# Three layers fused on one core: other step counts in a weight preparation, four combinations on another engine, a first fetch three units later

## The chip, the cores and the metric

The program runs on one core of a Trainium2 chip. Its time is the device time of one execution in microseconds (us), the median of several; 830.21 us is the median of three runs of the kernel before (829.67 to 830.74). The engines are TensorE (PE in the rows, its weight loads PEld), VectorE (DVE), ScalarE (ACT), GpSimd (POOL) and SyncE (SP), which here issues nearly all DMAs. Each engine works through its own instructions in the order in which the program wrote them; between engines there are semaphores.

## The reference, cut to what matters

```
scores = q @ k^T / 8 ;  ret = scores * gamma[h]**(i-j) for i>=j, else 0 ;  x = ret @ v    # 4 batches, 8 heads, 576 tokens, 64 wide
h = x @ w_in  ; x = (h * tanh(log1p(exp(h)))) @ w_out       # 2304 tokens, 512 -> 2048 -> 512 (Mish)
h = x @ w_in2 ; y = (h * sigmoid(1.702 h)) @ w_out2         # the same sizes (GELU by a sigmoid)
```

All of it in float32. The kernel gets there with reduced-precision float32 products: every operand is split into a high part and the rest, and three products stand for one.

## The kernel before, in words

**Retention** (`attention`) goes over 20 units, a batch and a chunk of up to 128 tokens each, `u` = 0 to 19. A unit's q, k, v come by one DMA of 1 MB into one of six buffers. `scores(u)` multiplies q and k on TensorE and masks on VectorE (`pm`), `decay_v(u)` scales v by powers of gamma on GpSimd, `update` and `take` renew the state, `outputs` and `finish` give the unit's part of X, which stays in SBUF.

**The first layer** (`first_layer`) takes the first 768 tokens in 32 slots, and in the meantime converts the weights. They arrive as raw 64-bit numbers, a chunk `m` of 16 at a time: VectorE clamps (`clamp`), ScalarE rescales (`rest`, `rebase`), VectorE puts the sign in (`sign`), GpSimd joins (`join`), ScalarE makes the high part and VectorE the low one (`convert`). Two chunks are one round `r`; when its second is converted, `combine_first` makes four sums and differences of the round's quarters (tile `cy`), splits them too, and writes them to DRAM (`first_stream`) by DMA. The other tokens go through the same layer by seven instead of eight quarter products (lines 1105 to 1200), in two passes of 120 steps each, with operands read back from `first_stream` through a ring. The last product of a slot is waited for by an activation on ScalarE and a subtraction on VectorE.

**The preparation** of the second layer's weights runs beside those passes and the start of the second layer: 32 pieces (`prepare`), one begun every 6.5 steps, 14 in the first pass, 14 in the second, 4 in the second layer's first steps. A piece goes through the same stages as above and is written to the DRAM tile `stream`; its tiles are called `cr` (raw) and `cy` (the seven quarters), or `X` where they lie in a free part of X.

**What sets the order.** The order is written by hand. A job is a generator; `plan` gives it the position at which it begins, and `position(name, step)`, called at fixed places of each step, lets every job that waits at `name` go on to its next yield. A `yield "skip"` costs one step, `pause(n)` is `n` of them, and `yield "vector"`, `"act early"` or `"pool"` goes on at that engine's place of the same step or the next. So the number of skips between two stages is the number of steps by which the second stands later in its engine's queue. `EARLY_AT` gives the unit in which each of the first two chunks is fetched and that in which its conversion begins.

The helpers through which most instructions go have lines of their own in the rows: L132 is every ScalarE activation, L475 every VectorE `tt`, L141 and L213 `sign`, L201 `clamp`, L217 `join`, L270 the four combinations of `combine_first`, L342 those of `prepare`, L275 and L352 VectorE's low parts behind them, L851 `decay_v`, L1135 and L1072 the two passes' products, L671 and L720 the second layer's.

Of the kernel before, what the change touches and what calls it, by code (L numbers as in the profile page):

```python
# [14 lines left out]
ALU = mybir.AluOpType  # L15
# [3 lines left out]
B, H, S, D = 4, 8, 576, 64  # L19
# [29 lines left out]

KEPT = (0, 1, 2, 3, 4, 8, 9, 10, 11, 12)  # L50
X_UNITS = (4, 5, 6, 7, 10, 11, 12, 13)
EARLY_AT = ((0, 5), (7, 13))
EARLY = len(EARLY_AT)
LATE = [-2 + 1.95 * i for i in range(NM - EARLY)]
LENT = (2, 11, 12)
# [2 lines left out]
TABLES = NCH * H + NPAIR * (NCH + len(GROW) + GROW[0])  # L58
FIRST = 4 * DM + (TABLES + 15) // 16 * 16
REST = CH[-1][1]  # L60
LAST = 2 * NPAIR * REST + DM


# [36 lines left out]
def retention_mish_gelu_kernel(ctx: ExitStack, tc: tile.TileContext, qkv, w1, w2, first_unit, rests, out):  # L100
    nc = tc.nc
# [153 lines left out]
    def combine_first(r):  # L255

        live["first"] = 1
        c, w = r * NP, W[0, r]
        for p, h, q in ((1, 0, 0), (2, 0, 1), (4, 1, 1)):
            nc.sync.dma_start(  # L260
                out=first_stream[:, c + R_ORDER.index(p)],
                in_=w[:, h, :, q * 2 * P : (q + 1) * 2 * P].bitcast(F32),
            )
        a11, a12, a21, a22 = (words(held[0, r])[3][:, q] for q in range(4))
        both = temp[0].tile([P, 8, 2 * P], F32R, tag="cy", name="cy")
        hi, y = both[:, :4], both[:, 4:].bitcast(F32)
        at = R_ORDER.index(6)
        s1, s2, s3, s4 = (y[:, R_ORDER.index(p) - at] for p in (5, 6, 7, 3))
        for o, a, b, op in ((s1, a21, a22, ALU.add), (s3, a11, a21, ALU.subtract), (s2, s1, a11, ALU.subtract), (s4, a12, s2, ALU.subtract)):
            nc.gpsimd.tensor_tensor(out=o, in0=a, in1=b, op=op)  # L270
        yield "pool"
        yield "act early"
        act(hi, y)
        yield "vector"
        nc.vector.tensor_tensor(out=both[:, 4:], in0=y, in1=hi.bitcast(F32), op=ALU.subtract)  # L275
        for j, t in enumerate((hi.bitcast(F32), y)):
            nc.sync.dma_start(out=first_stream[:, c + at : c + at + 4, j], in_=t)
        yield "vector"
        live["first"] = 0

    def pause(n):

        for _ in range(n):
            yield "skip"

    def prepare(j, r, part, half):

        late_one = j - sum(PREPARED_IN[:2])
        s = 0 if late_one >= 0 else R_ROUNDS[j >= PREPARED_IN[0]]
        while live["cr"] == 3:  # L290
            yield "skip"
        live["cr"] += 1
        if late_one >= 0:
            raw = idle(0, late_one % 3 * 2 * DM, 2 * DM)
        elif j % 3 == 2:
            raw = idle(s, 4 * DM, 2 * DM)
        else:
            raw = keep.tile([P, 2 * DM], F32, tag=f"x{2 + j % 3}", name="cr")
        raw = raw.rearrange("p (q n) -> p q n", q=4)
        nc.sync.dma_start(out=raw.bitcast(I32), in_=w2[r, part, half].bitcast(I32))  # L300
        yield from pause(7)
        yield "vector"
        clamp(raw)
        yield "act early"
        rest(raw)
        yield "act early"
        rebase(raw, nc.scalar)
        yield "skip"
        yield "vector"
        sign(raw)  # L310
        yield "pool"
        while live["cy"] == 3:
            yield "pool"
        live["cy"] += 1
        order = (UP_ORDER, DOWN_ORDER)[part]
        n = NP * 2 * P
        if late_one == 3:
            y = idle(0, 2 * DM, n).bitcast(F32R)
        elif late_one in (0, 1):
            at = NM - 2 + late_one  # L320
            y = place(at).tile([P, n], F32R, tag=f"w{at}", name="cy")
        elif late_one == 2 or j % 3 == 1:
            y = keep.tile([P, n], F32R, tag="side", name="cy")
        elif j % 3 == 0:
            y = temp[0].tile([P, n], F32R, tag="cy", name="cy")
        else:
            y = idle(s, 0, n).bitcast(F32R)
        y = y.rearrange("p (o a n) -> p o a n", a=2, n=P)
        v = y[:, :, 1].bitcast(F32)
        a11, a12, a22, s1, s2, s3, s4 = (order.index(p) for p in (1, 2, 4, 5, 6, 7, 3))  # L330
        a21 = s3

        bits = y[:, :, 1].bitcast(I32)
        join(raw[:, 0:2], bits[:, a11 : a21 + 1 : a21 - a11])
        join(raw[:, 2:4], bits[:, a12 : a22 + 1 : a22 - a12])
        for o, a, b, op in (
            (s1, a21, a22, ALU.add),
            (s3, a11, a21, ALU.subtract),
            (s2, s1, a11, ALU.subtract),
            (s4, a12, s2, ALU.subtract),  # L340
        ):
            nc.gpsimd.tensor_tensor(out=v[:, o], in0=v[:, a], in1=v[:, b], op=op)  # L342
        yield from pause(3)
        live["cr"] -= 1
        yield "skip"
        yield "act early"

        hi = y[:, :, 0]
        act(hi, v)
        yield from pause(2)  # L350
        yield "vector"
        nc.vector.tensor_tensor(out=y[:, :, 1], in0=v, in1=hi.bitcast(F32), op=ALU.subtract)  # L352
        yield from pause(2)
        c, step = (r * NP, 1) if part == 0 else (UP_STEPS + r, NR)
        nc.sync.dma_start(
            out=stream[:, c : c + (NP - 1) * step + 1 : step, half],
            in_=y.rearrange("p o a n -> p o (a n)").bitcast(F32),
        )
        prepared.add((r, part, half))
        yield from pause(8)  # L360
        live["cy"] -= 1

    n_u = len(UNITS)
# [8 lines left out]

    for m, (loaded_in, converted_in) in enumerate(EARLY_AT):
        plan("fetch", loaded_in - n_u, fetch(m))
# [410 lines left out]
    def attention():  # L785
        with tc.tile_pool(name="att", bufs=1) as ap:
# [11 lines left out]
            def load(u):  # L798

                b, c = UNITS[u]  # L800
                if c == NCH - 1:
                    t = ap.tile([P, LAST], F32, tag="rest", name="rest", bufs=2)
                    nc.sync.dma_start(out=t, in_=rests[b])
                    loaded[u] = views(t, REST)
                    return
# [9 lines left out]
            for t in (state[1][:, 0], state[1][:, 1:]):  # L815
# [6 lines left out]
            vt = tab[:, : NCH * H].rearrange("p (c h) -> p c h", c=NCH)  # L822
# [10 lines left out]
                out=cm, in_=cm, pattern=[[1, P]], compare_op=ALU.is_ge, fill=0.0, base=0, channel_multiplier=-1  # L833
# [13 lines left out]
            def decay_v(u):  # L847
                b, c = UNITS[u]
                n = CH[c][1]
                vv = loaded[u][2][:n].rearrange("p (h d) -> p h d", d=D)  # L850
                nc.gpsimd.tensor_tensor(  # L851
                    out=vv, in0=vv, in1=vt[:n, c, :].unsqueeze(2).to_broadcast([n, H, D]), op=ALU.mult
                )

            def scores(u):
                n = CH[UNITS[u][1]][1]
# [77 lines left out]
            def finish(u, o):  # L934
# [4 lines left out]
                while part < n:  # L939
# [6 lines left out]
                    )  # L946
                    part += w

            scores(0)
            decay_v(0)  # L950
            act(gt[:, 0, :, : GROW[0]], first)
            for j, w in enumerate(GROW):
                for p in range(NPAIR):
                    act(gt[:, 0, p, w : 2 * w], gt[:, 0, p, :w], scale=grow[:, p, j : j + 1])
            for u in range(n_u):
                step = u - n_u
                if u - 1 in wide and wide.index(u - 1) + len(buffers) < len(wide):
                    n = wide[wide.index(u - 1) + len(buffers)]
# [14 lines left out]
                o = outputs(u, before)  # L973
                if u == 1:
                    scores(u + 1)
                if u < NCH - 1:
                    n = CH[u + 1][1]
# [286 lines left out]
```

## Time and profile before

| what | value |
|---|---|
| median of three runs | 830.21 us |
| profiled execution: its own time, its span | 833.2 us, 831.5 us |
| TensorE matmul busy | 808.3 us, 97% of the span |
| VectorE, ScalarE, GpSimd busy | 582.3, 444.2, 220.3 us |
| mean granted TensorE clock | 0.995 |
| DMA | 219.67 MB, 264 GB/s |

The span begins with the first instruction and ends with the last. TensorE's sum is busy for all but some 23 us, so the rows to read are those on its waits. The stages lie in the span so: retention from 0 to about 73 us, the first layer's first 768 tokens to about 200, the two passes to 474, the second layer to the end. A wait of several semaphores is put down to the one that came last.

### The profile page before, as it was taken

To read this page: it belongs to the slowest core of one execution; us is meant where nothing else is said; L and a number is where in the kernel's file an instruction comes from. 1 tells how busy PE (TensorE), PEld (TensorE's weight loads), DVE (VectorE), ACT (ScalarE), POOL (GpSimd) and SP (SyncE) were. 2 spreads that over 40 slices of the span, in tenths; PEclk is the share of its full clock that TensorE was granted. 3 is DMA by queue.
4 is the path that set the end of the run, shared out by engine and by line. 5 is a ranking of instruction groups with operands and counts; after the bars stand their busy time and mean duration, and the time that the engine had idled before them with its cause. 6 is when DMAs were issued, how large, how long until landed. Compare 5 with 4: busy or idle time off the path is not lost.

```text
span 831.5 us, 14152 instructions
## 1 busy us (share of the span) xinstructions
PE 808.3 (97%) x5392; PEld 762.5 (92%) x5392; DVE 582.3 (70%) x959; ACT 444.2 (53%) x861; POOL 220.3 (26%) x284
## 2 busy tenths in 40 slices
PE   8999999999998999999899998999999999999998
PEld 8898888888887998988789998999999999999998
DVE  4786999999565667366476577588655798455776
ACT  5445776676655566555665554456233664233542
POOL 3452565652355550155463023000000000000000
PEclk9999999999999999999999999999999999999999
DMA  9983577838778886588787499878877778877775
GB/s 360 420 342 118 194 253 250 275 114 258 261 272 281 304 289 230 181 297 290 274 309 249 164 314 352 296 246 281 307 247 259 255 263 278 294 245 261 253 265 168
DMA packets 86132, 219.67 MB, mean 264 GB/s; under 512 B 5808, under 2 KB 51888, under 8 KB 78768
## 3 DMA queue, kind: packets, MB, share of 16 engines
q1 hardware_dynamic: 85920, 218.56, 76.1%
q8 instruction: 43, 0.70, 0.3%
q10 hardware_dynamic: 144, 0.20, 0.1%
q14 instruction: 25, 0.20, 0.1%
HBM read 169.98 MB, written 48.76 MB: 263 GB/s over the span
## 4 chain that ended last, share of the span: by engine, by line
PE 50%; POOL 7%; ACT 5%; DVE 5%; DMA 3%; issue 1%; SPq 0%; POOLq 0%; DVEq 0%
PE p L720 21%; PE p L671 18%; PE acc L1072 6%; PE p L1135 5%; POOL cy L342 3%; POOL cy L217 2%; ACT X L132 2%; DMA ring<-first_stream 2%; POOL X L342 2%; ACT cy L132 1%; DMA ring<-stream 1%; ACT cr L132 1%; POOL X L217 1%; DVE cr L141 1%; DVE cy L352 1%
## 5 line engine op out<-in xcount | busy, mean ns | idle before, releaser
L671 PE MATMUL p<-xop,ring 128*128 128x384 f32 x1008 | 176.1, 334 | 3.6 <-DVE cs L475 2.1
L671 PEld LDWEIGHTS p<-xop,ring 128*128 128x128 f32 x1008 | 174.7, 188 | 4.5 <-DVE cs L475 4.5
L720 PE MATMUL p<-g,ring 128*128 128x384 f32 x1008 | 175.2, 334 | 0.0
L720 PEld LDWEIGHTS p<-g,ring 128*128 128x128 f32 x1008 | 174.8, 188 | 0.0
L1072 PE MATMUL acc<-g,w 128*128 128x512 f32 (+1 forms) x768 | 145.7, 339 | 1.3 <-DVE g L475 1.3
L1072 PEld LDWEIGHTS acc<-g,w 128*128 128x128 f32 x768 | 125.5, 190 | 19.1 <-DVE g L475 2.0
L1135 PE MATMUL p<-xop,ring 128*128 128x384 f32 x672 | 131.3, 340 | 9.3 <-ACT c L132 4.0
L1135 PEld LDWEIGHTS p<-xop,ring 128*128 128x128 f32 x672 | 115.4, 188 | 13.7 <-DVE c L475 6.0
L132 ACT ACTIVATE g<-cs 128x384 fp32r<-128x384 f32 x168 | 79.0, 517 | 60.3 <-PE p L720 60.0
L475 DVE TENSOR_TENSOR g<-cs,g 128x384 fp32r<-128x384 f32 x168 | 90.0, 554 | 26.7 <-ACT g L132 25.0
L132 ACT ACTIVATE cs<-cs 128x384 f32<-128x384 f32 x72 | 37.7, 526 | 106.2 <-DVE cs L475 106.1
L475 DVE TENSOR_TENSOR g<-c,g 128x384 fp32r<-128x384 f32 x64 | 39.5, 617 | 52.2 <-ACT g L132 52.1
L437 PE MATMUL acc<-g,w 128*128 128x512 f32 (+1 forms) x384 | 72.3, 337 | 0.0
L437 PEld LDWEIGHTS acc<-g,w 128*128 128x128 f32 x384 | 60.2, 190 | 7.6
L217 POOL TENSOR_TENSOR raw<-raw 128x512 int32<-128x512 int32 x32 | 38.1, 1190 | 74.9 <-DVE raw L213 60.3
L132 ACT ACTIVATE cy<-cy 128x896 fp32r<-128x896 f32 (+1 forms) x30 | 29.5, 982 | 46.5 <-POOL cy L342 27.6
L475 DVE TENSOR_TENSOR cs<-cs 128x384 f32<-128x384 f32 x96 | 53.4, 557 | 0.8
L342 POOL TENSOR_TENSOR cy<-cy 128x128 f32<-128x128 f32 x88 | 52.3, 604 | 5.2
L132 ACT ACTIVATE g<-c 128x384 fp32r<-128x384 f32 (+1 forms) x96 | 50.5, 526 | 3.9 <-PE acc L437 0.9
L217 POOL TENSOR_TENSOR cy<-cr 128x256 int32<-128x256 int32 x38 | 29.3, 791 | 77.8 <-DVE cr L213 70.6
L416 PE MATMUL h<-x,w 128*128 128x512 f32 x192 | 46.6, 392 | 0.9 <-ACT c L132 0.9
L132 ACT ACTIVATE raw<-raw 128x512 int32<-128x512 uint32 x64 | 41.4, 677 | 10.8 <-DVE raw L201 10.4
(92 smaller groups left out, 998.3 us busy)
## 6 DMA issues: line engine op xcount, KB each, us to landing
ring<-stream SPq DMA_DIRECT2D x112, 512.0 KB, 4.6
ring<-stream SPq DMA_DIRECT2D x28, 1024.0 KB, 4.8
stream<-cy SPq DMA_DIRECT2D x22, 896.0 KB, 4.6
raw<-w_dram SPq DMA_DIRECT2D x32, 512.0 KB, 7.7
unit<-qkv_dram SPq DMA_DIRECT2D x15, 1024.0 KB, 10.8
ring<-first_stream SPq DMA_DIRECT2D x14, 1024.0 KB, 7.0
ring<-first_stream SPq DMA_DIRECT2D x28, 512.0 KB, 6.0
cr<-w_dram SPq DMA_DIRECT2D x19, 512.0 KB, 5.7
```

The lines of the kernel that those rows point to most:

```text
L132: nc.scalar.activation(out=o, in_=i, func=f, scale=scale, bias=bias)
L141: nc.vector.scalar_tensor_tensor(out=o, in0=i0, scalar=s, in1=i1, op0=op0, op1=op1)
L217: nc.gpsimd.tensor_tensor(out=o, in0=upper, in1=bits, op=ALU.add)
L342: nc.gpsimd.tensor_tensor(out=v[:, o], in0=v[:, a], in1=v[:, b], op=op)
L352: nc.vector.tensor_tensor(out=y[:, :, 1], in0=v, in1=hi.bitcast(F32), op=ALU.subtract)
L416: nc.tensor.matmul(h[:, :n], lhsT=W[0, m // 2][:, m % 2, a, k * P : (k + 1) * P], rhs=xs[t, k][:, b, :n], start=((k, a, b) == order[0]), s ...
L437: nc.tensor.matmul(acc[t, e][:, :n], lhsT=W[1, m // 2][:, m % 2, a, e * P : (e + 1) * P], rhs=g[:, b, :n],  start=(begins(i) and a == 0 an ...
L475: eng.tensor_tensor(out=o, in0=a, in1=b, op=op)
L671: nc.tensor.matmul(banks[p], lhsT=w[:, k, a * P : (a + 1) * P], rhs=x[:, b, k], start=(p not in SAME and k == 0 and a == 0 and b == 0), st ...
L720: nc.tensor.matmul(banks[e, p], lhsT=w[:, e, a * P : (a + 1) * P], rhs=g[:, b], start=(p != 2 and r == 0 and a == 0 and b == 0), stop=(r = ...
L1072: nc.tensor.matmul(acc[t, e][:, :w], lhsT=W[1, m // 2][:, m % 2, a, e * P : (e + 1) * P], rhs=g[:, b, o : o + w], start=(m == 0 and a == 0 ...
L1135: nc.tensor.matmul(bank, lhsT=w[:, a, k * P : (k + 1) * P], rhs=x[:, b, k], start=(p in (1, 2, 7) and k == 0 and a == 0 and b == 0), stop= ...
```

## The change

It has five parts. (1) `EARLY_AT`: the first chunk of weights is fetched at unit 2 instead of 0 and converted from unit 8 instead of 5. (2) `decay_v` of unit 0 is shared: five heads (320 columns) on VectorE and three (192) on GpSimd, and it is written ahead of `scores(0)`. (3) `combine_first`: its four combinations are VectorE's, and the `yield "pool"` behind them is gone. (4) `prepare`: 6 skips instead of 7 between the fetch and the clamp; 2 instead of 1 between ScalarE's rescaling and VectorE's sign; 5 instead of 3 behind GpSimd's combinations (with the one that stays, 6 instead of 4 up to ScalarE's split); 1 instead of 2 between ScalarE's split and VectorE's low part; 7 instead of 8 up to the buffer's release. (5) A constant `SPLIT` for part 2, by which the lines below it move by one.

```diff
-EARLY_AT = ((0, 5), (7, 13))
+EARLY_AT = ((2, 8), (7, 13))
+SPLIT = 5
@@ combine_first
-            nc.gpsimd.tensor_tensor(out=o, in0=a, in1=b, op=op)
-        yield "pool"
+            nc.vector.tensor_tensor(out=o, in0=a, in1=b, op=op)
         yield "act early"
@@ prepare
-        yield from pause(7)
+        yield from pause(6)
         yield "vector"
         clamp(raw)
...
         rebase(raw, nc.scalar)
-        yield "skip"
+        yield from pause(2)
         yield "vector"
         sign(raw)
...
-        yield from pause(3)
+        yield from pause(5)
         live["cr"] -= 1
         yield "skip"
         yield "act early"
         hi = y[:, :, 0]
         act(hi, v)
-        yield from pause(2)
+        yield "skip"
         yield "vector"
         nc.vector.tensor_tensor(out=y[:, :, 1], in0=v, in1=hi.bitcast(F32), op=ALU.subtract)
         yield from pause(2)
...
-        yield from pause(8)
+        yield from pause(7)
         live["cy"] -= 1
@@ decay_v
-                nc.gpsimd.tensor_tensor(
-                    out=vv, in0=vv, in1=vt[:n, c, :].unsqueeze(2).to_broadcast([n, H, D]), op=ALU.mult
-                )
+                for eng, h, e in ((nc.vector, 0, SPLIT), (nc.gpsimd, SPLIT, H)) if u == 0 else ((nc.gpsimd, 0, H),):
+                    by = vt[:n, c, h:e].unsqueeze(2).to_broadcast([n, e - h, D])
+                    eng.tensor_tensor(out=vv[:, h:e], in0=vv[:, h:e], in1=by, op=ALU.mult)
@@ attention
+            decay_v(0)
             scores(0)
-            decay_v(0)
```

TensorE's order does not change. SyncE's queue during retention, from the load of unit 4 (`rest`) on; `unit` tiles are retention's buffers, `raw` the first chunk of weights. Before:

```order
L803 DMA rest<-rests_dram 128x1024
L811 DMA unit<-qkv_dram 128x2048
L183 DMA raw<-w_dram 128x512 x2
L811 DMA unit<-qkv_dram 128x2048
L811 DMA unit_77<-qkv_dram 128x2048
L811 DMA unit_78<-qkv_dram 128x2048
```

Now:

```order
L803 DMA rest<-rests_dram 128x1024
L811 DMA unit<-qkv_dram 128x2048 x2
L811 DMA unit_77<-qkv_dram 128x2048
L811 DMA unit_78<-qkv_dram 128x2048
L803 DMA rest<-rests_dram 128x1024
L184 DMA raw<-w_dram 128x512 x2
```

The two fetches of the first chunk stood ahead of the load of unit 6 and of three loads behind it; now they stand behind unit 9's.

ScalarE's queue at the first two preparations of the first pass; `cr` and `X` of 128x512 are the two rescalings of a piece, `cy` of 128x7x128 its split, `c` and `g` belong to the first layer. Before:

```order
L132 ACTIVATE c<-p 128x384
L132 ACTIVATE cy<-cy 128x7x128
L132 ACTIVATE cr<-cr 128x512 x2
L132 ACTIVATE c<-p 128x384
L132 ACTIVATE c<-c 128x384
L132 ACTIVATE g<-c 128x384
L132 ACTIVATE c<-p 128x384
L132 ACTIVATE cy<-cy 128x7x128
L132 ACTIVATE X<-X 128x512 x2
```

Now:

```order
L133 ACTIVATE cr<-cr 128x512
L133 ACTIVATE c<-p 128x384
L133 ACTIVATE cr<-cr 128x512
L133 ACTIVATE cy<-cy 128x7x128
L133 ACTIVATE c<-p 128x384
L133 ACTIVATE c<-c 128x384
L133 ACTIVATE g<-c 128x384
L133 ACTIVATE X<-X 128x512
L133 ACTIVATE c<-p 128x384
L133 ACTIVATE X<-X 128x512
L133 ACTIVATE cy<-cy 128x7x128
```

The rescalings of the next piece stood behind the split of the piece ahead of it, and now stand in front of it.

VectorE's queue in the first layer, at the first round's combinations; L457 makes the low part of an activation, L249 that of a weight. Before:

```order
L457 TENSOR_TENSOR g<-c,g 128x256
L249 TENSOR_TENSOR w_1190<-raw,w_1190 128x512
L141 SCALAR_TENSOR_TENSOR raw<-raw 128x512
L213 TENSOR_SCALAR raw<-raw 128x512
L201 TENSOR_SCALAR raw<-raw 128x512
L457 TENSOR_TENSOR g<-c,g 128x512
L275 TENSOR_TENSOR cy<-cy 128x1024
```

Now:

```order
L457 TENSOR_TENSOR g<-c,g 128x256
L271 TENSOR_TENSOR cy<-raw 128x256 x2
L271 TENSOR_TENSOR cy<-cy,raw 128x256
L271 TENSOR_TENSOR cy<-raw,cy 128x256
L250 TENSOR_TENSOR w_1191<-raw,w_1191 128x512
L142 SCALAR_TENSOR_TENSOR raw<-raw 128x512
L214 TENSOR_SCALAR raw<-raw 128x512
L202 TENSOR_SCALAR raw<-raw 128x512
L457 TENSOR_TENSOR g<-c,g 128x512
L275 TENSOR_TENSOR cy<-cy 128x1024
```

Four instructions of 256 columns are added to VectorE in each of eight rounds, between two low parts of activations, and GpSimd's queue loses them.

## Rows read from the trace of the kernel before

**Rows 1.** TensorE by stretch: stretch, length, busy (matmuls), granted clock, DMA share, GB/s
```profile
8.00:60.00 52.00, 50.14 (x938) 0.97 0.98 403
60.00:200.00 140.00, 138.83 (x923) 1.00 0.61 200
...
206.00:320.00 114.00, 109.53 (x608) 0.99 0.82 284
...
346.00:430.00 84.00, 78.74 (x439) 1.00 0.80 281
...
480.00:530.00 50.00, 46.44 (x265) 1.00 0.97 351
530.00:828.00 298.00, 297.89 (x1719) 1.00 0.77 260
```
**Rows 2.** TensorE's waits, 206 to 430 us: total, times, longest
```profile
PE p L1135 <- DVE c L475: 3.9, 9, 0.9
PE p L1135 <- ACT c L132: 3.1, 4, 1.1
PE p L1135 <- DMA ring<-first_stream: 1.5, 2, 0.9
PE acc L1072 <- DVE g L475: 1.3, 2, 0.7
```
**Rows 3.** TensorE by stretch, columns as in Rows 1
```profile
24.00:30.00 6.00, 6.00 (x86) 0.72 1.01 419
266.00:272.00 6.00, 5.37 (x22) 0.72 0.96 335
```
**Rows 4.** Timeline of retention: start, length, engine, what, [idle before <- releaser]
```profile
4.14 1.06 SPq L183 DMA_DIRECT2D raw<-w_dram  x2
...
5.93 1.29 DVE L866 TENSOR_TENSOR pm<-sc,cm 128x512 f32<-128x512 f32 x2 [4.47 <-PE sc L862]
...
7.18 0.69 PE L885 MATMUL ds<-unit 128*64 128x64 f32 x16 [1.35 <-POOL unit L851]
...
23.99 1.21 PE L862 MATMUL sc<-unit 64*128 64x128 f32 x16 [1.61 <-DMA unit<-qkv_dram]
```
**Rows 5.** Timeline of the first layer, and VectorE's 256-column group (mean ns)
```profile
150.60 1.34 DVE L141 SCALAR_TENSOR_TENSOR raw<-raw 128x512 int32<-128x512 int32 x1
...
153.48 1.06 ACT L132 ACTIVATE cy<-cy 128x1024 fp32r<-128x1024 f32 x1 [3.19 <-POOL cy L270]
...
156.57 0.68 DVE L141 SCALAR_TENSOR_TENSOR raw<-raw 128x512 int32<-128x512 int32 x1
...
156.76 3.02 PE L416 MATMUL h<-x,w 128*128 128x512 f32 x12 [0.90 <-ACT c L132]
...
L403 DVE TENSOR_TENSOR side<-X,side 128x256 fp32r<-128x256 f32 x4 | 1.8, 462 | 0.0
```
**Rows 6.** Waits of ScalarE and VectorE, 206 to 430 us
```profile
ACT cy L132 <- POOL cy L342: 22.1, 16, 3.4
...
ACT X L132 <- POOL X L342: 10.0, 6, 3.4
...
DVE cy L352 <- ACT cy L132: 8.9, 7, 1.9
...
DVE X L352 <- ACT X L132: 4.7, 4, 1.9
```
**Rows 7.** Timeline of the first pass at one such wait
```profile
261.45 0.95 ACT L132 ACTIVATE cy<-cy 128x896 fp32r<-128x896 f32 x1 [3.39 <-POOL cy L342]
...
264.90 1.33 PE L1135 MATMUL p<-xop,ring 128*128 128x384 f32 x6 [1.08 <-ACT c L132]
```
**Rows 8.** Second layer's start: TensorE's waits 480 to 530 us, then the timeline
```profile
PE p L671 <- DVE cs L475: 2.1, 2, 1.4
PE p L671 <- DMA ring<-stream: 1.5, 1, 1.5
...
501.18 0.69 DVE L141 SCALAR_TENSOR_TENSOR X<-X 128x512 int32<-128x512 int32 x1 [1.16 <-ACT X L132]
```

## The prediction

> **What bounds the kernel now.** I read TensorE by stretch first, since its sum is busy for 97% of the span. From 530 to 828 us it is busy for 297.89 of 298 us [rows 1]: nothing can be won there. What it loses lies in four places: 1.9 us from 8 to 60 us, 1.2 us from 60 to 200, 4.5 us from 206 to 320 and 5.3 us from 346 to 430 (the two passes), and 3.6 us from 480 to 530 (the second layer's start) [rows 1]; each is length less busy. To these comes the clock. In two stretches of six us the mean granted clock is 0.72 [rows 3]: part of each ran at the lower level, 1.2 GHz, and 6 x 0.28 = 1.7 us of work at 2.4 GHz were lost in each. Both follow on idle time of TensorE, the first on the 1.61 us at 23.99 us [rows 4], the second on the 1.08 us at 264.90 us [rows 7] and another short wait behind it.
>
> Next come the waits, to see who ended that idle time. In retention it is a DMA, unit 6's load [rows 4]. In the two passes 3.9 + 3.1 + 1.3 = 8.3 us are put down to VectorE's and ScalarE's work on activations and 1.5 us to ring loads [rows 2]; in the second layer 2.1 us to VectorE and 1.5 us to a ring load [rows 8].
>
> The engines behind them are not short of time there but stand in line. ScalarE waits 22.1 + 10.0 = 32.1 us, in 22 cases, for GpSimd's combinations in front of a piece's split [rows 6]. One case shows what this does: ScalarE sits idle for 3.39 us, the activation parts queued behind it come late, and TensorE sits idle for 1.08 us until one of them is there [rows 7]. Since the next piece's rescaling also stands behind that split, its sign, its join and its combinations come late too, and the piece after meets the same wait.
>
> **The change part by part.** The sum is made against the profiled execution, 833.2 us with a span of 831.5; that lies 3.0 us above the median of 830.21, and I take the sum off the median.
>
> *First chunk later.* Two fetches of 512 KB are issued at 4.14 us, ahead of unit 6's load [rows 4]. DMA moves 403 GB/s in this stretch, at a share of 0.98 [rows 1], so the 1.05 MB take 2.6 us out of unit 6's way. It is awaited for 1.61 us [rows 4]: the wait goes, with 1.0 us to spare, and units 7 to 9 come earlier by the same 2.6 us. Without this idle time I expect the clock not to fall: 1.7 us. Together 3.3 us (0 to 3.3). What is moved: the two DMAs, and for each of them eight instructions of the conversion, four of VectorE, three of ScalarE and one of GpSimd. They now lie between units 8 and 12, whose VectorE work is lighter because the first split of X is over; the second chunk begins at unit 13 as before. The DMAs are queued ahead of unit 10's load as they were, so from there on nothing comes later. Cover is needed on VectorE alone: were it gone, one unit's mask (1.29 us [rows 4]) would be late.
>
> *Unit 0's decay shared.* TensorE waits 1.35 us for it, to 7.18 us [rows 4]. 320 columns on VectorE take about 0.5 us, between 0.46 for 256 and 0.68 for 512 columns [rows 5]. But VectorE now does this ahead of the two masks, which last 1.29 us from 5.93 us [rows 4] and cannot begin before the tables have landed: they end about 0.6 us later, at 7.8 us, and the outputs need them. What the state gains, the outputs wait for. I take 0 (0.5 lost to 0.5 won): units 1 to 3 land behind one another and set the pace anyway.
>
> *Combinations on VectorE.* Added to VectorE: 8 rounds x 4 x 0.46 us [rows 5] = 14.8 us, in the stage where it has hardly any idle time. Against it: beside GpSimd's combinations the same VectorE instruction lasts 1.34 us and alone 0.68 [rows 5]. Per round two instructions of this kind stand beside them, 1.3 us, and two shorter ones, so that 1.3 us or somewhat more come back for 1.85 us added. ScalarE's wait of 3.19 us in front of the split, which made TensorE wait 0.90 us [rows 5], becomes one for VectorE's 1.85 us. I take all of the 1.2 us lost in the stage [rows 1] as won, and no loss, as TensorE's products use an activation only three slots after it was made. From both sides: 1.2 us won to 14.8 lost.
>
> The Trainium skill (SBUF — State Buffer, "Who interferes with whom") has it that a VectorE instruction with two SBUF inputs contends with a GpSimd instruction that reads SBUF, and that the loser blocks in full. The rows agree on the contention but show a doubling, 1.34 against 0.68 us. By the rule VectorE would get back all of GpSimd's time and gain on the whole; by the rows it loses about 0.5 us a round, and as TensorE does not wait for it there, the sum is the same.
>
> *Preparation.* In steps of about one product group, GpSimd now has six instead of four before ScalarE asks, and the next piece's rescaling is in front of the split. A step is about 1.1 us (274 us for two passes of 120 steps), two steps more are 2.3 us, and the 22 waits are 1.5 us in the mean [rows 6]; the longest, 3.4 us, come from a piece that was itself late. So I take it that the 32.1 us of ScalarE's waiting go. One wait may stay: VectorE's low part has one step instead of two behind the split, and it already waited 8.9 + 4.7 = 13.6 us with two [rows 6]. Of the two kinds of waiting, 32.1 of 45.7 us go, 0.70, and I take that share of TensorE's 8.3 us: 5.8 us (0 to 8.3). The ring loads stand behind the write of a piece on SyncE, and that write waits for the low part; with the low part on time I take half of the 1.5 us [rows 2], 0.7 (0 to 1.5). The second stretch at a low clock goes with its wait: 1.7 us (0 to 1.7). A fetch now has six steps to land instead of seven, a reason not to take more.
>
> *Second layer's start.* The wait at 501.18 us, VectorE's sign for a rescaling that stood behind the split [rows 8], is of the same kind and made the longer of the two waits, 1.4 us [rows 8]; it goes, the shorter one, VectorE's own backlog, stays. The ring load that TensorE waited 1.5 us for [rows 8] stood behind the last piece's write on SyncE; in the new order it stands ahead of it, and I take the 1.5 us as won. Together 2.8 us (0 to 3.6).
>
> Sum: 3.3 + 0 + 1.2 + 5.8 + 0.7 + 1.7 + 2.8 = 15.5 us, so **814.7 us**. With every wait gone (3.3 + 1.2 + 8.3 + 1.5 + 1.7 + 3.6 = 19.6, and 0.5 of unit 0) it would be 810.1.
>
> **The rivals.** *Waits that change places.* VectorE's low part, now one step behind, waits for ScalarE at every piece and holds the activation parts behind it; the passes give back a third of the 8.3 us, the low clock stays, as do the ring loads, and the second layer gives half. 3.3 + 1.2 + 2.8 + 1.4 = 8.7: 821.5 us. For it: 11 such waits, up to 1.9 us, with two steps [rows 6]. Against it: those came behind a split that was itself late.
>
> *Nothing arrives.* Retention's 3.3 us are taken back at the first layer, which needs weights that are loaded when retention's buffers come free, and the passes are bound by ring loads, at a DMA share of 0.82 [rows 1], so that activation waits turn into DMA waits: 829 to 831 us. Against it: from 530 to 828 us TensorE has no wait with ring loads at a share of 0.77 [rows 1].
>
> *VectorE becomes the first layer's bound, and the kernel slower.* Nothing of the contention comes back, the added 1.85 us per round reach TensorE in all 8 rounds (14.8 us), and each such wait, about as long as the 1.61 us of retention, is followed by 1.7 us lost to the clock, as there (13.6 us). Less the other gains, 14.3 us, this is 14.1 us slower: 844.3 us. It decides from the point where VectorE's work of a round is longer than TensorE's, so that the lag of three slots is used up. For it: VectorE's idle time in this stage is small; against it: the doubling [rows 5], which shows that part of its busy time is waiting for GpSimd. The Trainium skill (Perfetto Trace Analysis, "Optimizing Scalar/DVE Operations") warns that moving work between these two engines might not help as they share a port; no row here shows the moved work.
>
> **How the numbers follow.** Forecast 0.66, around 809.5 to 819; changed places 0.20, 819 to 826; nothing 0.07; slower 0.07. What a measurement can tell from no change is about 0.2%, 1.7 us. Faster: 0.66 + 0.20 and a little of the third, 0.87; same 0.06; slower 0.07. The range runs from the end where every wait is gone, a little below it, to the upper end of the second case: 809 to 826.
>
> **What would show it.** In the profile after: unit 6's scores without a wait and a clock of 1.00 from 24 to 30 us; no ScalarE wait for L271 over 2 us and TensorE busy throughout 60 to 200 us; ScalarE's waits for GpSimd's combinations in the passes under 8 us instead of 32; TensorE's waits from 206 to 430 us under 4 us and a clock of 1.00 around 266 us; no wait for a ring load near 528 us. I am wrong if VectorE's waits for ScalarE's split grow beyond 14 us, if low parts of activations come later than three slots in the first layer, or if the time won in retention shows again as a wait of the first slots.

## The result, and the profile after

Median of the kernel after: 811.07 us (810.31 to 812.1, four runs); of the kernel before beside it: 830.48 us (829.67 to 832.0, four runs). The ratio is 0.9765, with an interval of 0.9747 to 0.9783, that is 19.5 us less (18.0 to 21.0). The forecast was 814.7 us in a range of 809 to 826. The profiled execution took 810.9 us with a span of 809.2; against the profiled execution of before that is 22.3 us less, some 3 us more than by the medians, since that execution of before (833.2 us) was itself 2.7 us above this median; it held two stretches at the lower clock [rows 3].

TensorE by stretch in the kernel after (stretch, length, busy, granted clock, DMA share, GB/s), to be read against [rows 1]:

```profile
8.00:60.00 52.00, 51.95 (x1000) 1.00 0.98 403
60.00:200.00 140.00, 140.00 (x893) 1.00 0.66 213
206.00:320.00 114.00, 113.96 (x652) 1.00 0.85 288
346.00:430.00 84.00, 82.14 (x469) 1.00 0.91 309
480.00:530.00 50.00, 48.81 (x279) 1.00 0.91 328
530.00:806.00 276.00, 275.60 (x1590) 1.00 0.78 261
```

The stretches in which TensorE lost time are nearly full, and what is left sits in two of them: 1.9 us from 346 to 430 and 1.2 us from 480 to 530. Who is waited for there is read from TensorE's waits, first 206 to 430 us, then 480 to 530 us (total, times, longest), to be read against [rows 2, 8]:

```profile
PE p L1135 <- DMA ring<-first_stream: 1.9, 1, 1.9
...
PE p L671 <- DMA ring<-stream: 0.8, 1, 0.8
PE p L671 <- DVE cs L475: 0.4, 1, 0.4
```

Of 15 waits for VectorE and ScalarE in the two passes none is left. Of ring loads one wait is left, and it is longer than the two of before together (1.9 us instead of 1.5).

*Retention.* SyncE's first chunk, the start, and unit 6's scores in the timeline after, against [rows 4]:

```profile
6.03 0.49 DVE L853 TENSOR_TENSOR unit<-unit 128x320 f32<-128x320 f32 x1 [4.56 <-DMA unit<-first_unit_dram]
...
6.57 0.81 PE L885 MATMUL ds<-unit 128*64 128x64 f32 x16 [0.88 <-DVE unit L853]
...
13.34 1.65 SPq L184 DMA_DIRECT2D raw<-w_dram  x2
...
22.31 1.16 PE L862 MATMUL sc<-unit 64*128 64x128 f32 x16
```

Unit 6's scores have no bracket: nothing is waited for, 1.68 us earlier than before. The two stretches that ran partly at 1.2 GHz [rows 3] have their answer here; the work of the second lies some 13 us earlier now:

```profile
24.00:30.00 6.00, 6.00 (x118) 1.00 1.01 388
...
254.00:260.00 6.00, 6.00 (x36) 1.00 0.82 283
```

*The preparation.* The waits of ScalarE and VectorE from 206 to 430 us, against [rows 6]:

```profile
ACT cy L133 <- POOL cy L342: 3.1, 5, 1.1
...
DVE cr L142 <- ACT cr L133: 2.5, 3, 0.9
...
DVE cy L352 <- ACT cy L133: 1.1, 4, 0.3
...
ACT X L133 <- POOL X L342: 0.8, 3, 0.4
...
DVE X L352 <- ACT X L133: 0.6, 2, 0.3
```

ScalarE's waits for GpSimd fell from 32.1 to 3.9 us. VectorE's waits for the split (L352), which the forecast left standing, fell from 13.6 to 1.7 us. The case picked out ahead of the prediction, a split 3.39 us late and TensorE idle for 1.08 us behind it [rows 7], has no successor: the longest of ScalarE's waits for GpSimd is 1.1 us. How the two hang together can be read from the trace of before: ahead of 13 of TensorE's 15 waits for activations from 206 to 430 us, at most 6 us earlier, ScalarE waited 0.8 to 3.4 us for GpSimd in front of a split, and ahead of the other two VectorE waited 1.07 and 1.06 us for a rescaling.

*First layer.* VectorE's combinations are L271. From 60 to 206 us, columns TensorE, its loads, VectorE, ScalarE, GpSimd (busy and count), clock, DMA share, GB/s; before:

```profile
60.00:206.00 146.00, 143.95 (x953) 126.64 (x950) 136.30 (x176) 97.71 (x173) 70.63 (x63) 1.00 0.63 203
```

and after, with two groups of VectorE's instructions in it (mean ns of one last):

```profile
60.00:206.00 146.00, 146.00 (x927) 129.58 (x923) 131.15 (x210) 101.81 (x179) 33.80 (x29) 1.00 0.67 217
...
L142 DVE SCALAR_TENSOR_TENSOR raw<-raw 128x512 int32<-128x512 int32 x28 | 19.1, 683 | 0.7 <-ACT raw L133 0.7
...
L271 DVE TENSOR_TENSOR cy<-raw 128x256 f32<-128x256 f32 x16 | 6.0, 415 | 1.6 <-DMA first_stream<-cy 1.6
```

VectorE executes 32 combinations more (16 of them are the row above; all 12.7 us), and yet it is busy for 5.2 us less. The group L142, 28 instructions, lasts 683 ns in the mean; before it was L141, with 846 ns, a mixture of durations such as 0.68 and 1.34 us [rows 5]:

```profile
L141 DVE SCALAR_TENSOR_TENSOR raw<-raw 128x512 int32<-128x512 int32 x28 | 23.7, 846 | 0.8 <-ACT raw L132 0.8
```

### The profile page after: what moved, and what is told of

It is laid out like the page before. It is cut to its first block, busy times and chain, and to the rows that moved or that the text cites. A ratio compares the mean times of both kernels' runs of the same rounds, so it can differ in the third digit from the quotient of the medians.

```text
span 809.2 us, 14167 instructions
## 1 busy us (share of the span) xinstructions
PE 800.4 (99%) x5392; PEld 759.7 (94%) x5392; DVE 585.3 (72%) x992; ACT 445.7 (55%) x861; POOL 190.9 (24%) x252
## 4 chain that ended last, share of the span: by engine, by line
PE 94%; DMA 3%; DVE 2%; ACT 1%; issue 0%; SPq 0%
PE p L720 22%; PE p L671 19%; PE acc L1072 16%; PE p L1135 14%; PE h L416 8%; PE acc L437 8%; PE sc L862 2%; PE o L924 2%; PE o L913 2%; PE ds L885 1%; DMA ring<-first_stream 1%; DMA ring<-stream 1%; DMA unit<-first_unit_dram 1%; DVE cs L475 0%; DVE cy L352 0%
## 5 line engine op out<-in xcount | busy, mean ns | idle before, releaser
L475 DVE TENSOR_TENSOR g<-cs,g 128x384 fp32r<-128x384 f32 x168 | 90.1, 554 | 26.7 <-ACT g L133 25.0
L475 DVE TENSOR_TENSOR g<-c,g 128x384 fp32r<-128x384 f32 x64 | 44.3, 692 | 39.5 <-ACT g L133 39.0
L133 ACT ACTIVATE c<-p 128x384 f32<-128x384 f32 x64 | 31.3, 488 | 56.3 <-PE p L1135 56.0
L342 POOL TENSOR_TENSOR cy<-cy 128x128 f32<-128x128 f32 x88 | 54.7, 631 | 5.2
L475 DVE TENSOR_TENSOR cs<-cs 128x384 f32<-128x384 f32 x96 | 53.4, 556 | 0.8
L218 POOL TENSOR_TENSOR cy<-cr 128x256 int32<-128x256 int32 x38 | 31.6, 851 | 61.9 <-DVE cr L214 56.6
```

What stands on the lines that cost most here:

```text
L133: nc.scalar.activation(out=o, in_=i, func=f, scale=scale, bias=bias)
L218: nc.gpsimd.tensor_tensor(out=o, in0=upper, in1=bits, op=ALU.add)
L475: eng.tensor_tensor(out=o, in0=a, in1=b, op=op)
```

## The experiments

The theory: ScalarE's split of a piece arrives late because GpSimd's combinations have too few steps; all else in the passes (rescalings, low parts, ring loads) comes late behind it. The rival named in the forecast: the waits move to other places. A second rival came up on the way: the loop of split, rescaling and combination feeds on itself, so that any link broken frees it. All ratios are to the kernel before, run beside.

**One part of the change at a time.** Each is the kernel before with one part of the change.

First chunk later:

```diff
-EARLY_AT = ((0, 5), (7, 13))
+EARLY_AT = ((2, 8), (7, 13))
```

> The kernel before with the first chunk fetched at unit 2 and converted from unit 8, nothing else. Theory (each part takes away its own waits, TensorE keeps what it wins): unit 6's 1.61 us wait goes, the clock stays at its upper level from 24 to 30 us, and the time falls by 1.6 to 3.3 us. Rival (what retention wins is taken back where the first layer waits for its weights): the wait is gone, but TensorE's waits from 60 to 200 us grow from 1.2 us to 3 or more, and the time stays within 1 us.

Measured: 828.85 us, ratio 0.9968 (0.9957 to 0.998), 2.7 us. TensorE from 24 to 30 us:

```profile
24.00:30.00 6.00, 6.00 (x116) 1.00 1.02 397
```

The clock is full here and unit 6 is not waited for; the idle times behind it stood where they were, and in this execution the drop of the clock came in another place, near 525 us (below).

Unit 0's decay shared (`decay_v` in two parts, ahead of `scores(0)`):

> The kernel before with unit 0's decay shared between VectorE and GpSimd and written first, nothing else. Theory: within 0.5 us of the kernel before, since units 1 to 3 land at the same times; the 1.35 us wait at 7 us becomes one of about 0.9 us and a short one for the masks. Rival (the state comes earlier and all behind it): 0.5 to 1 us faster, with unit 3's scores starting earlier than 13.56 us.

Measured: 830.1 us, ratio 0.9995 (0.9984 to 1.0006): nothing. The wait of 1.35 us became two for the masks' outputs, and unit 6 was waited for as before, 1.40 us, though the clock did not fall behind it here:

```profile
7.70 0.43 PE L925 MATMUL o<-pm,unit 128*64 128x128 f32 x2 [0.24 <-DVE pm L867]
8.30 1.09 PE L925 MATMUL o<-pm,unit 128*64 128x128 f32 x14 [0.17 <-DVE pm L867]
23.98 1.16 PE L863 MATMUL sc<-unit 64*128 64x128 f32 x16 [1.40 <-DMA unit<-qkv_dram]
```

The combinations on VectorE:

```diff
-            nc.gpsimd.tensor_tensor(out=o, in0=a, in1=b, op=op)
-        yield "pool"
+            nc.vector.tensor_tensor(out=o, in0=a, in1=b, op=op)
```

> The kernel before with combine_first's four combinations on VectorE, nothing else. Theory: ScalarE's waits for the combinations (18.7 us, up to 3.2) fall under 8 us, TensorE's two waits of 1.2 us in 60 to 200 us go, and the time falls by about 1 us (0.1%), perhaps 2 with the wait at 203 us. Rival (VectorE becomes the bound of that stage): TensorE's waits from 60 to 200 us grow to 5 us or more and the kernel is slower.

Measured: 826.83 us, ratio 0.9946 (0.9933 to 0.996), 4.5 us: a miss, in size. TensorE is busy throughout 60 to 200 us, as expected, and behind it too:

```profile
200.00:206.00 6.00, 6.00 (x33) 1.00 0.96 348
```

In the kernel before TensorE waited 0.88 us there, at 203.75 us, for an activation behind the last round's split; the forecast, whose stretch ended at 200 us, had left it out. Nor are the 4.5 us all due to the combinations: the mean granted clock was 0.999 or 1.000 in all five executions of this kernel, and in about half of those of before it was lower. In the two traces TensorE's groups gain 3.0 us over the three waits.

The step counts alone (five numbers of the preparation):

```diff
-        yield from pause(7)
+        yield from pause(6)
...
-        yield "skip"
+        yield from pause(2)
...
-        yield from pause(3)
+        yield from pause(5)
...
-        yield from pause(2)
+        yield "skip"
...
-        yield from pause(8)
+        yield from pause(7)
```

> The kernel before with the step counts of the preparation alone. Theory: most of the change's gain: ScalarE's waits for GpSimd's combinations fall from 32 us to under 6, TensorE's waits in the two passes from 9.7 us to about 2 (a ring load), at the second layer's start from 3.6 to about 1.2, the clock stays up near 266 us; 12 to 16 us faster. Rival (the parts need each other: with retention and the first layer as before the passes start with a backlog): under 8 us faster.

Measured: 817.18 us, ratio 0.9828 (0.9808 to 0.9847), 14.3 us. From 204 to 530 us TensorE has two waits left, 2.21 us for a ring load and 0.39 us; all those for activations are gone. The four parts give 2.7 + 0.4 + 4.5 + 14.3 = 21.9 us against 19.5 of the whole; with intervals of about 1 us each the difference is not one that can be read.

**Which of the step counts does it.** The kernel before with the first two of the five edits (the next piece's rescaling ahead of the split):

> The kernel before with only one part of the new step counts: the next piece's rescaling and its reads come ahead of ScalarE's split (pause 7 to 6, and two steps in place of the skip), while ScalarE still asks four steps after GpSimd began its combinations. Theory (slack: what arrives too late is GpSimd's combination, so the number of steps behind it decides): ScalarE's waits for GpSimd in the two passes stay above half of the 33 us that they have in the kernel before between 200 and 440 us, and the time falls by a third to a half of the 14.3 us that all step counts together gave: 823 to 826 us, ratio 0.991 to 0.994. Rival (order: the loop of split, rescaling and combination feeds on itself, and whichever stands first breaks it): nearly all of the 14 us, 816 to 819 us, and the waits for GpSimd fall below 10 us although the steps are the old ones.

Measured: 819.17 us, ratio 0.9862 (0.9846 to 0.9879), 11.5 us. And with the last three (the split two steps later, the rescaling where it was):

> The kernel before with only the other part of the step counts: ScalarE's split waits two steps more behind GpSimd's combinations (pause 3 to 5, one step fewer behind the split, and the release after 7 steps instead of 8), while the rescaling of the next piece stays where it was. Theory (slack): nearly all of the 14.3 us of all step counts, 816 to 820 us, with ScalarE's waits for GpSimd between 200 and 440 us below 8 us. Rival (order): the rescaling still stands behind the split, comes late with it, and the combinations begin late: waits of 10 to 20 us stay, and the time falls by at most 7 us, to 823 us or more.

Measured: 816.07 us, ratio 0.9821 (0.9806 to 0.9836), 14.9 us. The waits from 206 to 430 us, of the first of these two:

```profile
ACT cy L132 <- POOL cy L342: 13.7, 15, 2.8
...
ACT X L132 <- POOL X L342: 7.1, 7, 2.7
DVE cy L352 <- ACT cy L132: 6.7, 4, 2.3
...
DVE cr L141 <- ACT cr L132: 2.8, 3, 0.9
...
PE p L1135 <- DVE c L475: 0.5, 2, 0.3
```

and of the second:

```profile
DVE cr L141 <- ACT cr L132: 7.1, 8, 1.5
...
DVE cy L352 <- ACT cy L132: 2.7, 6, 1.3
...
ACT X L132 <- POOL X L342: 2.3, 4, 0.8
...
ACT cy L132 <- POOL cy L342: 1.8, 3, 0.8
```

The theory was right on the waits of both and wrong on the time of the first. With the rescaling ahead of the split and the four steps kept, ScalarE still stands idle for 20.8 of 32.1 us for GpSimd, and yet TensorE's waits for activations in the passes fall from 8.3 us to 0.5. So the late split alone does not make TensorE wait. What went beside it is VectorE's waiting for the rescaling of the next piece (L141), 2.8 us here and 10.6 in the kernel before:

```profile
DVE cr L141 <- ACT cr L132: 10.6, 8, 3.6
```

That this is why TensorE no longer waits fits the rows, but was not tested apart. With the split later, the rescaling is still behind it (7.1 us), but the split is on time, and no wait of TensorE for an activation is left in the passes. Either cut frees the loop; the second one alone gives all that both together give. That is the second rival's picture for the time, and the theory's for where each cut acts.

**How much room has VectorE.** The kernel after, with each combination executed twice:

```diff
-            nc.vector.tensor_tensor(out=o, in0=a, in1=b, op=op)
+            for _ in range(2):
+                nc.vector.tensor_tensor(out=o, in0=a, in1=b, op=op)
```

> The kernel after with each of the four combinations of a first layer's round executed twice on VectorE, the second time with the same result: 8 x 4 x 0.46 = 14.8 us more of VectorE's work between 60 and 206 us. Theory (VectorE's work of the first layer lies beside TensorE's, and there is room for this much again, since GpSimd no longer contends): TensorE stays busy for at least 139 of the 140 us from 60 to 200, the time is within 1.7 us of the kernel after, 811 to 813 us. Rival (VectorE is at the edge there, the case of VectorE as the bound): TensorE waits for VectorE's activations for 5 to 15 us in this stretch, 816 to 826 us.

Measured: 823.1 us, ratio 0.9908 (0.9892 to 0.9924), 11.9 us slower than the kernel after by the ratios (0.0143 of 830.5). The theory fell: there is no room for as much again. TensorE by stretch, then one round of the timeline:

```profile
60.00:200.00 140.00, 134.28 (x842) 1.00 0.60 196
...
153.09 1.07 ACT L133 ACTIVATE cy<-cy 128x1024 fp32r<-128x1024 f32 x1 [2.46 <-DVE cy L272]
...
157.20 2.97 PE L417 MATMUL h<-x,w 128*128 128x512 f32 x10 [1.29 <-ACT c L133]
```

ScalarE waits 2.46 us for VectorE's combinations, and TensorE 1.29 us for the activation behind the split. Up to 128 us TensorE's groups start no later than in the kernel after; from there to 210 us they fall 11.5 us behind, of 13.6 us added. From 114 to 131 us VectorE is busy for 16.7 of 17 us, in the kernel after for 16.8: it was full there already, and the room is some 2 us in the whole stage. This is the first half of the slower rival of the forecast at work; it decides between once and twice the added 13 us. Its second half, a fall of the clock behind each wait, did not come: the clock is 1.00. That it did not decide at once fits what VectorE got back from GpSimd: it has 131.15 us of work in 146, and by an estimate, with the 17.2 us found below added, would have had 148 without.

**The combinations taken out of the whole.** The kernel after with its first layer's combinations back on GpSimd:

> The kernel after with the first layer's combinations back on GpSimd (as in the kernel before), everything else changed. Theory: what the combinations on VectorE bring is TensorE's idle time from 60 to 206 us (0.91 + 0.27 + 0.88, some 2.1 us), and no more when the other parts are there: 813 us, ratio to the kernel before 0.979. Rival (the 4.5 us that this part alone gave are its own worth, with something beyond the waits): 815.5 us, and then the profile shows a longer stretch somewhere else than in 60 to 206 us, or a stretch at a lower clock.

Measured: 814.76 us, ratio 0.9808 (0.9793 to 0.9823), so the combinations are worth 3.6 us there, between the two expectations. Since all else is equal, this is also the comparison for VectorE's time (columns as above):

```profile
60.00:206.00 146.00, 144.09 (x908) 126.74 (x905) 135.61 (x176) 98.80 (x174) 67.68 (x61) 1.00 0.65 211
```

With the combinations VectorE is busy for 131.15 us, 12.7 of them theirs, so 135.61 - 131.15 + 12.7 = 17.2 us came back, half of the 67.68 - 33.80 = 33.9 us that GpSimd spent. TensorE's idle time from 60 to 206 us is 0.85 + 0.25 + 0.80 = 1.9 us; one of these in the timeline:

```profile
198.17 1.21 PE L1136 MATMUL p<-xop,ring 128*128 128x384 f32 x6
200.18 1.33 PE L1136 MATMUL p<-xop,ring 128*128 128x384 f32 x6 [0.80 <-ACT c L133]
201.35 1.55 PE L438 MATMUL acc<-g,w 128*128 128x512 f32 x6
```

and the same twelve matmuls in the kernel after:

```profile
196.46 2.25 PE L1135 MATMUL p<-xop,ring 128*128 128x384 f32 x12
198.55 1.55 PE L437 MATMUL acc<-g,w 128*128 128x512 f32 x6
```

From the first of them to the next group it is 201.35 - 198.17 = 3.18 us with the wait and 198.55 - 196.46 = 2.09 us without: the wait of 0.80 us costs 1.09. The 0.29 us more stand as busy time: six matmuls at a time last 1.21 and 1.33 us in the records, half of the twelve 1.13. Over the three waits the same group starts 2.8 us later than in the kernel after (201.35 against 198.55). The rest, 1.0 us in these two traces, came behind 394 us, where a wait of 2.21 us was followed by the lower clock (below), as the rival had named it. So 2.8 us are the combinations' own, 1.9 of them idle time.

**Unit 0's decay taken out of the whole** (the kernel after with `decay_v` and the masks as before):

> The kernel after without the shared decay of unit 0 and with the masks' old place. Theory: as in the kernel before the units' loads set the pace up to unit 3, the time is that of the kernel after within 0.5 us, 810.5 to 811.6 us, though the first wait is longer (1.1 to 1.5 us instead of 0.88). Rival (without unit 6's wait behind it, nothing levels out the loss of the start): 0.3 to 0.6 us slower than the kernel after, and every later stretch is that much later.

Measured: 811.6 us, ratio 0.9769 (0.9755 to 0.9783), 0.3 us from the kernel after and far inside the intervals. TensorE's wait for unit 0's decay was 1.23 us instead of 0.88, and at unit 2 the two kernels are level. The length of this wait is not the part's doing alone: over the traces of the kernels with the old decay it goes from 0.34 to 1.47 us, with the new one from none to 1.17.

**The wait that is left.** SyncE's issues and TensorE's products around 391 us in the kernel after:

```profile
380.80 0.37 SPq L355 DMA_DIRECT2D stream<-X  x1
381.22 0.55 SPq L300 DMA_DIRECT2D X<-w_dram  x1
381.87 3.47 SPq L1016 DMA_DIRECT2D ring<-first_stream  x2
...
391.05 1.28 PE L1135 MATMUL p<-xop,ring 128*128 128x384 f32 x6 [1.86 <-DMA ring<-first_stream]
```

The ring load of 1 MB is issued behind a write of 896 KB and a fetch of 512 KB, both issued in the microsecond ahead of it, and lands 9.05 us later. It is also issued late. SyncE's own waits, in the kernel after from 374.3 to 382 us, and then in the kernel with the write one step later (next) from 376 to 380 us:

```profile
SPq L355 <- DVE X L352: 6.4, 1, 6.4
...
SPq L1016 <- PE p L1135: 3.7, 1, 3.7
```

In the kernel after SyncE stands for 6.4 us at the write, whose data VectorE has not finished, with the ring load behind it in its queue. With the write behind the ring load, SyncE waits for the load's buffer alone and issues it at 378.16 us, some 3 us earlier against TensorE's work; it lands 5.1 us later.

Two kernels move the write by a step. Later:

```diff
-        yield from pause(2)
+        yield from pause(3)
         c, step = (r * NP, 1) if part == 0 else (UP_STEPS + r, NR)
...
-        yield from pause(7)
+        yield from pause(6)
```

> The kernel after with the write of a prepared piece one step later (3 steps behind the low part in place of 2; the buffer's release stays where it was). Theory (the 1.86 us that TensorE waits at 391 us are the ring load's, which stands behind the write of 896 KB issued 1.1 us ahead of it): the ring load is issued ahead of that write and lands some 2 us earlier, the wait goes, and with it the second layer's 0.80 us at 493 us or not: 808 to 809.5 us, TensorE busy 83.5 us or more of the 84 from 346 to 430. Rival (DMA is full in this stretch, share 0.91, so that an exchange of two transfers makes another one late): a wait of 1 to 2 us for another ring load or for an activation in its place, 810.5 to 812 us.

Measured: 808.8 us (807.4 to 811.21), ratio 0.9734 (0.9714 to 0.9754). The wait is gone:

```profile
346.00:430.00 84.00, 84.00 (x480) 1.00 0.91 315
```

Against the kernel after, the groups in front of it start 0.5 us earlier and those behind it 2.6 us. By the ratios this version is 2.6 us below the kernel after; the two intervals overlap at their edge, so the order of the two rests on the trace as much as on the times. And earlier (the same two pauses, a skip and 8):

> The kernel after with the write of a prepared piece one step earlier (1 step behind the low part in place of 2; the release unchanged). Theory (the write stands in front of the ring load): it starts 1.1 us earlier, the ring load behind it lands up to 1.1 us earlier, the wait at 391 us falls from 1.86 to 0.8 us: 809.5 to 811 us. Rival (the write now waits for VectorE's low part, and the queue of SyncE stands still with the fetch and the ring load behind it): SyncE waits for L352 more than once, the wait at 391 us stays or grows, 811 to 814 us.

Measured: 813.36 us, ratio 0.979 (0.9773 to 0.9807). As the rival had it, the ring load's wait grew, to 2.10 us, and SyncE waited 130 us for low parts (L352) instead of 110: the write in question leaves no earlier against TensorE's work, since it waits for its low part. But of the 2.5 us by which this trace is behind, 1.8 arose in retention, which is the same in both kernels; what the write alone costs stays open.

## Why the prediction was right, point by point

- *First chunk later, 3.3 us.* Right: 2.7 us alone (1.7 to 3.6), but with some clock in it: between the executions with a mean granted clock of 0.999 or more it is 1.4 us (830.3 to 828.9). In the two profiles 3.4 us are there by 42 us, 1.7 of them idle time and what goes with it, 1.7 the clock; the part put down to the clock holds for that execution only. (The fetch moved by two units and the conversion by three; in SyncE's queue the fetch stands four loads later.)
- *Unit 0's decay, 0.* Right, with the reason given: 0.4 us (-0.5 to 1.3) alone, 0.3 in the whole.
- *Combinations, 1.2 us.* The mechanism was right, the size less than half: 2.8 to 3.0 us over the three waits in three pairs of traces; the medians have 4.5 us alone and 3.6 in the whole, with some of the clock in both. The 0.88 us at 203.75 us was not counted, since the stretch that I had read ended at 200 us; and a wait costs more than its idle time. What came back on VectorE was mis-sized as well. I took 10.4 us (8 rounds x 1.3); it was 17.2 us (17.9 by the rows of before and after). By the Trainium skill (SBUF — State Buffer, "Who interferes with whom") the shared ports are an exclusive lock, and issue order decides which of the two engines blocks. That is no rule by which VectorE blocks every time, as the prediction read it, and the rows show that half of GpSimd's time came back, not all. The sentence cited for the slower rival (the Trainium skill, Perfetto Trace Analysis, "Optimizing Scalar/DVE Operations"), that such a move might not help, was no bar here: the move helped, and only the same work executed twice cost time.
- *Preparation, 5.8 + 0.7 + 1.7 us.* **This is the term that was off.** "One wait may stay", VectorE's low part, and from it the share of 0.70, was wrong: I read 13.6 us of VectorE's waiting as a consequence of its two steps, and it was a consequence of the late split, as the waits after show. All 8.3 us went. A share of the waits was the wrong measure anyway: with the new place of the rescaling alone 20.8 of ScalarE's 32.1 us stayed, and 7.8 of TensorE's 8.3 us went. The ring loads gave nothing (1.5 us became 1.9); the half that I took rested on the low part being on time for the write, and at 381 us a ring load stands behind a write that waits 6.4 us for it. With the second layer's start I had 11.0 us; alone the step counts gave 14.3.
- *Second layer's start, 2.8 us.* Right in size (2.6 us in the two traces; 3.6 us of idle time became 1.2), not in its parts: of the two waits for VectorE it was the shorter, 0.74 us, that went, and the longer fell from 1.35 to 0.39; the ring load that was awaited at 528 us is on time, but another one, 72 matmuls ahead of it, is waited for for 0.80 us.
- *The sum.* 15.5 us against 19.5. TensorE's order is the same in both kernels, so the starts of its groups can be compared one by one: the kernel after is ahead by 3.4 us behind retention, 6.4 at 206 us, 19.7 at the end of the passes and 22.3 at 536 us. By stage these are 3.4, 2.9, 13.3 and 2.6 us against a forecast of 3.3, 1.2, 8.2 and 2.8. By kind: TensorE's waits in the profile are 27 before in the whole span, 19.5 us together, and 6 after, 5.15 us; 14.4 us of idle time are gone, and 2 x 1.7 = 3.4 us are the two stretches at the lower clock. That makes 17.8 of the 22.3 us. The other 4.5 us, over 21 waits gone, are 0.2 us each: the restart, which no row of idle time holds. The group starts show it wait by wait: 0.90 us of idle time at 156.76 us cost 1.20, 0.88 at 203.75 cost 1.18, 0.35 at 238.05 cost 0.59. A forecast by "every wait gone" was therefore no upper end either.
- *The clock's 3.4 us.* In these the sum was lucky. They were read from one execution with two such stretches and taken off a median that holds less of them: of 35 executions of the kernel before beside the experiments, 17 have a mean granted clock of 0.999 or 1.000, with a median of 830.3 us, and three of the four of the kernel after, with 810.9. That is 19.4 us without the clock, where the forecast's other terms made 12.1. And the stretch near 267 us was no loss of its own: three kernels that waited there as long (1.1 and 0.6 us) without a fall of the clock, the kernel before with the first chunk, the decay or the combinations alone changed, had won some 1.5 us on it behind that place, and had given them back by 291 us of its span in longer waits for activations.
- *The signs named ahead.* All came out (unit 6 without a wait, both clocks at 1.00, ScalarE's 3.9 us under the 8, TensorE's 1.9 us under the 4, no wait for the load of 528 us); but another ring load is waited for in the second layer, 0.8 us at 493 us.
- *The rivals.* Changed places: VectorE's waits for the split did not grow (13.6 to 1.7 us). Others of its waits did, for ScalarE's and TensorE's part of an activation (L475 for `c`, 5.0 to 22.5 us), and cost nothing: VectorE now stands ready for them. Nothing arrives: retention's 3.4 us are all there up to 150 us, where the first wait of the first layer stood, and only one transfer took the place of activations, for 1.9 us. VectorE as the bound: its mechanism is real at twice the work, not at once.

## What to carry to other kernels

Where engines hand one piece of work around a loop, a wait seen at several links may have one cause: count the links before keeping a share of the waits, and cut the loop at the cheapest place. In this kernel a wait of TensorE cost its idle time and some 0.2 to 0.3 us of restart beside it. Read a stage a few microseconds past its end, and take a clock term off the execution in which it was read, not off a median. When compute waits are gone, look at what stands ahead of the next awaited load in the queue that issues it, and what that waits for.

## What the runs showed of the hardware that was not expected

The drop of TensorE's clock is not tied to one wait of a kernel. The kernel before had it behind the waits of 1.61 and 1.08 us [rows 3, 4, 7]. Six-microsecond stretches behind waits of other kernels, first the combinations on GpSimd again (a wait of 2.21 us), then the first chunk alone (2.09 us):

```profile
393.00:399.00 6.00, 4.79 (x19) 0.72 0.97 353
...
524.00:530.00 6.00, 5.06 (x20) 0.72 0.48 197
```

and the kernel after behind its wait of 1.86 us, then the step counts alone behind 2.21 us:

```profile
390.00:396.00 6.00, 4.95 (x28) 1.00 1.00 353
...
395.00:401.00 6.00, 5.16 (x30) 1.00 0.89 329
```

A wait of the same line and the same 2.21 us was followed by the lower level in one execution and not in the other. Over all traces, waits of 1.86 to 2.30 us for a ring load come eight times and are followed by it twice; the pair of 1.1 and 0.6 us in the passes comes eight times in the kernel before and three others, and is followed by it twice; unit 6's waits of 1.61 and 1.62 us were followed by it, those of 1.22, 1.24, 1.40 and 1.43 us were not. What decides it is not shown by these rows; a gain from it can be expected on the mean, not assigned to a place. It is one part of the spread of the times: the executions of the kernel before with a mean clock of 0.999 or 1.000 have a median of 830.3 us, the others one of 831.6. It is not the only one: the kernel with the later write has 807.4 to 811.21 us, all at 1.000.
